# A two-layer kernel on one core: the skip term added by TensorE, more turns by DMA, and a new written order

## The chip, the cores and the metric

The kernel runs on one core of one Trainium2 chip. The metric is the device time of one execution in microseconds (us). Before the change three runs took 256.9 to 257.2, with a median of 257.14.

## The reference

Two kinds of layer alternate, twice each, on x of 2048 tokens by 512 channels (x starts as q). `LN` is a layer norm without weights.

```python
def A(q, k, v, shift_k, ssm_k, ssm_D):
    k_shift = sum(shift(k, t) * shift_k[:, t] for t in range(4))   # causal, 4 taps per channel
    kv = k_shift * v
    y = causal_conv(kv, ssm_k)          # per channel, length 2048, by FFT of 4096 points
    y = y + kv * ssm_D
    return q * y

def B(x, w1, b1, w2, b2):               # 512 -> 1376 -> 512
    return gelu(LN(x) @ w1 + b1) @ w2 + b2

for _ in range(2):
    x = x + A(LN(x), k, v, shift_k, ssm_k, ssm_D)
    x = x + B(LN(x), w1, b1, w2, b2)
```

k, v, the filter and D are the same in both A layers, so y is the same too: the kernel computes it once and keeps it.

## The kernel before

All of A's heavy work is in a first part of about 98 us; the rest is the four layers' norms and gates and two MLPs (`mm1` at L704, `mm2` at L738; four groups of four token tiles, two passes), which the change does not touch.

The first part computes the long convolution as a transform of 32 x 64 points by matmuls. Names of the steps, with c a group of 128 channels (0 to 3):

- `lk`, `lv`, `lK`, `lx` and others on S (SyncE's queue): loads. `lsT` brings the short filter's taps, `sF` (POOL) converts them, and `dg0` to `dg2` (L435, four operations each) make diagonal matrices `DG` from them.
- `kT0` to `kT3` (PE, L441) turn four blocks of k; `kT0e` to `kT3e` copy them out of PSUM.
- `kv{c}{o}` (PE, L524) apply the four taps by the diagonals for groups 0 to 2; `kvm` (DVE, L530) multiplies by v. Group 3 is done by POOL: `kg0` to `kg3` and `ka1` to `ka3` (L455, L457, L462), then `kgm` (L466).
- `s00` (statistics of the first four token tiles), `s01` (POOL, small) and `s02` (its normalisation, four operations): the first norm.
- `kd0`, `kd4` (L393): D is added to the filter's first tap, `Kd[:, :, 0]`, from `Dz`, for each half of the filter.
- `KS` (PE, L400, 16 blocks) and `K2` (PE, L413, 16 blocks) transform the filter; `sa`, `sb` (S) copy its halves to the other row order. Together the K stage.
- `U{c}S{q}` (PE, L325) is the first stage for kv, `U{c}T{h}` its turn: by PE and a copy (L357), or by a DMA transpose (L304), as the string `UT` says for each group (`P` or `X`).
- For each group and j from 0 to 3: `X` (PE, L558, second stage), `T` (DVE, L573, product with the filter), `V` (PE, L582, inverse second stage).
- `Z` (DMA transposes, L629) and `TC`, `TD` (PE, L617) turn the result, `Y` (PE, L649) is the last stage, and `g`, `h`, `p`, `b`, `LT0` gate, normalise and turn the first token tiles for the MLP.

A name with `e` is the emptying of that block's PSUM bank pair, by ACT (L237) or DVE (L239). PSUM has four such slots. What runs where, and in what order, is a list written out by hand, `ORDER`: `name.engine` and the slots taken (P for PE, D for VectorE, A for ScalarE, G for GpSimd, S for SyncE's queue). `_Plan.write` issues the steps in that order, so each engine and SyncE's queue work their own steps strictly in it. The costs and dependences in `plan.add` served to find the order; the semaphores follow from the memory that the issued instructions touch.

Of the kernel before, what the change touches and what calls it, by code (L numbers as in the profile page):

```python
# [28 lines left out]
sa0.S U2T0.P3 K27e.A K213.P2 K25e.A U2T1.P0 K213e.A sa1.S U1T0.P1 U2T0e.D B1.G sb1.S s11.G U2T1e.A sb3.S  # L29
U3S0.P22 sa3.S U1T0e.D U1T1.P3 U3S0e.A X20.P00 U1T1e.D U3S2.P1 X20e.A X10.P21 U3S2e.D X21.P32 X10e.A U3S3.P0  # L30
T20.D0 X21e.A U3S1.P1 U0T0.P2 lx.S U3S1e.A T10.D1 X13.P30 U3S3e.A V20.P10 U0T0e.D X13e.A U3T0.S X23.P01 T21.D2
U0T1.P2 V20e.A T13.D0 X00.P32 X23e.A V10.P11 U0T1e.D X00e.A V21.P0 V10e.A T23.D1 X01.P30 V13.P2 V21e.A T00.D2
X02.P11 X01e.A V23.P0 X02e.D V13e.A X03.P32 T01.D0 V23e.A V00.P1 X03e.A T02.D1 X11.P20 V01.P0 V00e.A T03.D2
X12.P31 X11e.A V02.P1 V01e.D X12e.A U3T1.S X30.P22 T11.D0 V02e.A V03.P0 X30e.A T12.D1 X22.P30 V11.P1 V03e.A
T30.D2 X31.P21 X22e.A Z01.S V12.P0 V11e.D X31e.A Z00.S T22.D0 X32.P32 V12e.A V30.P12 X32e.A T31.D1 Z10.S
X33.P20 V22.P0 X33e.A T32.D2 Z03.S V31.P3 V22e.A T33b.D0 V32.P2 Z13.S V31e.A T33a.D1 V33b.P0 V30e.D V32e.A
Z02.S V33a.P3 V33be.D V33ae.A TC0a.P1 TC0b.P2 Z12.S TC0ae.A TD0a.P3 TC1.P0 TC0be.D TD0ae.A Z11.S TD0b.P1
TC1e.D Y00.P2 TD0be.A TC3.P3 w3.S w1.S Y00e.A g00.D w2.S Y01.P1 TC3e.A w4.S TC2.P0 g01.D Y02.P2 h00.D Y01e.A
# [87 lines left out]
def kernel(ctx: ExitStack, tc: tile.TileContext, A_q, A_k, A_v, A_shift_k, A_ssm_k, A_ssm_D,  # L126
                 B_x, B_w1, B_b1, B_w2, B_b2, out):
    nc = tc.nc
    P = 128
# [166 lines left out]
    with tc.tile_pool(name="ps", bufs=1, space=bass.MemoryType.PSUM) as ps:  # L296
# [92 lines left out]
        for c in range(8):  # L389
            if c % (8 // NK) == 0:  # L390
                sl = slice(c * 16, c * 16 + P // NK)
                kd = plan.add(f"kd{c}", {"G": 300, "D": 130}, lK[c * NK // 8], lambda it, sl=sl: (
                    nc.vector if it["eng"] == "D" else nc.gpsimd).tensor_tensor(Kd[:, sl, 0], Kd[:, sl, 0], Dz[:, sl], ALU.add))  # L393
# [433 lines left out]
```

## Time and profile before

| | us |
|---|---|
| median of three runs | 257.14 |
| the profiled execution | 256.81 |
| its span, first to last instruction | 255.1 |
| TensorE busy | 236.8 |
| VectorE busy | 174.5 |
| ScalarE busy | 146.1 |
| GpSimd busy | 54.5 |
| first matmul of the MLP begins at | 97.9 |

In the rows that follow, `L393` is a line of the kernel, `out<-in` are tiles (nearly all of them lie in one big tile, `arena`), `x4` a count, and a bracket at the end tells how long the engine had been idle before and what ended that. A time alone is counted from the span's start. The granted clock is TensorE's, as a part of full speed.

### The profile page before, as it was taken

The page shows a single profiled execution, that of the slowest core. Times are in us where ns is not written, and L with a number is a line of the kernel's source. Part 1 is how long each engine was busy: PE and PEld are TensorE (multiplying, and loading weights), DVE is VectorE, ACT ScalarE, POOL GpSimd, SP SyncE. Part 2 cuts the span into 40 slices and gives each one's busy share as a digit, 9 for nine tenths or more (in the row PEclk, how much of TensorE's full clock was granted, in tenths as well). Part 3 has the DMA queues.
Part 4 walks back from the last instruction along what each step waited for, and adds up shares of the span by engine and source line. Part 5 has one row for each costly group of instructions (what it writes and reads, how often), then busy time and mean ns, then how long its engine had stood idle before and what let it go on. Part 6 is the DMA issues. An engine that isn't in the chain of part 4 may idle for free.

```text
span 255.1 us, 5088 instructions
## 1 busy us (share of the span) xinstructions
PE 236.8 (93%) x2084; PEld 146.3 (57%) x2084; DVE 174.5 (68%) x321; ACT 146.1 (57%) x210; POOL 54.5 (21%) x52
## 2 busy tenths in 40 slices
...
GB/s 132 382 334 167 222 442 180 76 320 321 312 135 103 148 237 288 3 0 82 5 82 0 78 6 20 62 0 82 4 1 165 0 11 157 0 14 71 1 20 63
DMA packets 53040, 30.15 MB, mean 118 GB/s; under 512 B 46642, under 2 KB 50456, under 8 KB 51736
## 3 DMA queue, kind: packets, MB, share of 16 engines
...
## 4 chain that ended last, share of the span: by engine, by line
PE 72%; DVE 12%; DMA 7%; issue 4%; ACT 2%; SPq 2%; ACTq 0%; DVEq 0%
PE po L738 30%; PE ph L704 29%; DMA arena<-in_A_v_dram 4%; DVE T L573 4%; DVE arena L239 3%; PE p L325 2%; PE p L357 2%; PE p L649 2%; DVE arena L393 2%; DMA arena<-in_A_ssm_D_dram 2%; PE p L400 2%; PE p L413 2%; PE p L524 1%; DVE ZT L239 1%; DMA arena<-ZT 1%
## 5 line engine op out<-in xcount | busy, mean ns | idle before, releaser
L706 ACT ACTIVATE arena<-ph,B 128x512 bf16<-128x512 f32 (+5 forms) x110 | 63.7, 604 | 81.1 <-PE ph L704 81.0
L704 PE MATMUL ph<-arena 128*128 128x512 bf16 (+4 forms) x440 | 78.5, 336 | 0.1
L738 PE MATMUL po<-arena 128*128 128x512 bf16 (+2 forms) x363 | 77.4, 373 | 0.0
L704 PEld LDWEIGHTS <-arena 128*128 128x128 bf16 (+1 forms) x440 | 40.4, 100 | 37.2 <-DMA arena<-in_B_w_dram 0.4
L738 PEld LDWEIGHTS <-arena 128*128 128x128 bf16 (+1 forms) x363 | 35.4, 98 | 40.5
L743 DVE TENSOR_TENSOR arena<-po,arena 128x512 bf16<-128x512 f32 (+1 forms) x33 | 21.5, 673 | 43.6 <-PE po L738 43.6
L237 ACT ACTIVATE arena<-p 128x1024 bf16<-128x1024 f32 (+5 forms) x38 | 37.8, 1071 | 10.1 <-PE p L441 3.9
L271 POOL TENSOR_TENSOR lrsm<-lrsm,mhalf 128x4 f32<-128x4 f32 (+2 forms) x10 | 8.9, 885 | 95.9 <-DVE lrsm L265 95.9
L237 ACT ACTIVATE ZT<-p 128x1024 bf16<-128x1024 f32 (+1 forms) x22 | 22.0, 1055 | 2.5 <-PE p L325 2.5
L259 DVE BATCH_NORM_STATS2 lstm<-arena 128x6 f32<-128x512 bf16 x32 | 19.9, 681 | 0.2
L573 DVE TENSOR_TENSOR T<-xb,arena 128x2048 bf16<-128x2048 bf16 (+1 forms) x17 | 18.7, 1159 | 0.0
L239 DVE CAST arena<-p 128x1024 bf16<-128x1024 f32 x15 | 17.7, 1223 | 1.4 <-PE p L400 0.9
L582 PE MATMUL p<-arena,T 128*128 128x128 bf16 x256 | 16.5, 219 | 1.0 <-DVE arena L239 0.4
L271 POOL TENSOR_TENSOR lrsg<-lrsg,mhalf 128x4 f32<-128x4 f32 x8 | 8.1, 1014 | 40.2 <-DVE lrsg L268 40.1
L237 ACT ACTIVATE xb<-p 128x1024 bf16<-128x1024 f32 x15 | 16.1, 1165 | 0.1
L582 PEld LDWEIGHTS <-T 128*128 128x128 bf16 x256 | 14.9, 98 | 1.6 <-issue 1.3
L455 POOL TENSOR_TENSOR T<-arena,SK 128x2048 bf16<-128x2048 bf16 (+3 forms) x4 | 14.9, 3740 | 3.8 <-ACT arena L237 3.7
L259 DVE BATCH_NORM_STATS2 lstg<-arena 128x6 f32<-128x512 bf16 x24 | 14.8, 679 | 0.0
L276 DVE TENSOR_SCALAR arena<-arena,lmvg,lrsg 128x512 bf16<-128x512 bf16 x28 | 9.7, 409 | 6.7 <-POOL lrsg L271 6.7
L239 DVE COPY arena<-p 128x2048 bf16<-128x2048 bf16 (+3 forms) x10 | 10.5, 1049 | 4.4 <-issue 3.0
L276 DVE TENSOR_SCALAR arena<-arena,lmvm,lrsm 128x512 bf16<-128x512 bf16 x32 | 11.2, 409 | 2.3 <-POOL lrsm L271 2.3
L524 PE MATMUL p<-DG,arena 128*128 128x128 bf16 x192 | 11.4, 219 | 1.2 <-ACT ZT L237 0.9
...
## 6 DMA issues: line engine op xcount, KB each, us to landing
...
arena<-tabM SPq DMA_DIRECT2D x1, 2048.0 KB, 12.1
arena<-in_A_q_dram SPq DMA_DIRECT2D x1, 2048.0 KB, 8.2
...
```

The costliest lines, as they stand in the source:

```text
L237: nc.scalar.activation(dst, src, AF.Copy)
L239: nc.vector.tensor_copy(dst, src)
L259: nc.vector.bn_stats(self.st[:, i, 0, :], x_t[:, GT * g + i, :] if src is None else src[:, i, :])
L271: nc.gpsimd.tensor_tensor(self.rs[:, a:b], self.rs[:, a:b], mhalf[:, a:b], ALU.pow)
L276: nc.vector.tensor_scalar(out=dst[:, i, :], in0=xs, scalar1=self.mv[:, i, 0:1], scalar2=self.rs[:, i:i + 1], op0=ALU.subtract, op1=ALU.mult)
L455: nc.gpsimd.tensor_tensor(m[:, t:NT, :], kn[:, 0:NT - t, c3], sk(t, NT - t), ALU.mult)
L573: eng.tensor_tensor(view(Tb[it["slot"]["T"]], [2, n, CW]), x2, kk, ALU.mult)
L582: nc.tensor.matmul(o[:, i, :], T[:, r, i, :], Mt[:, ka + i, 1 - r, :], start=r == 0, stop=r == 1)
L704: nc.tensor.matmul(o.rearrange("p (i t) -> p i t", t=P), W1t[:, ct, ft * P:ft * P + m], lt[:, a:b, ct, :], start=ct == 0, stop=ct == CT - 1)
L706: nc.scalar.activation(hT[0:m, ft, a * P:b * P], o, AF.Gelu_apprx_tanh, bias=B1[0:m, ft:ft + 1])
L738: nc.tensor.matmul(po[:, a:b], hT[0:m, ft, i * P:(i + 1) * P], W2t[0:m, ft, a:b], start=ft == 0, stop=ft == FT - 1)
L743: nc.vector.tensor_tensor(xs, po[:, a:b], xs, ALU.add)
```

## The change

1. `kd0` and `kd4` become two matmuls each on PE (identity by `Kd`'s column, identity by `Dz`, summed in PSUM) and an emptying back into `Kd`: `kd0e` on ACT, `kd4e` on DVE.
2. `UT` goes from `PPPX` to `PPXX`: group 2 of u is turned by two DMA transposes instead of 32 PE transposes and two copies.
3. The load of x, 2 MB, becomes four of 512 KB, `lr0` to `lr3`, later in SyncE's queue.
4. The weight loads' dependences in the plan name fewer products.
5. Some costs in the plan are changed (`kv` 1880, `s00` 6500 and `s02` 2900 on ACT).
6. The order is new throughout. Among other things `lsT` now stands behind the four loads of k, the blocks of k come as 1, 2, 0, 3 instead of 1, 3, 0, 2, `dg0` and `s02` change engine (ACT; DVE), and the groups of X, T and V come as 1, 0, 2, 3 instead of 2, 1, 0, 3. In the old list DVE's steps run, at the place that the prediction speaks of, `U2T0e U1T0e U1T1e U3S2e T20 T10 U0T0e T21 T13 U0T1e T23 T00 X02e T01 T02 T03 V01e T11 T12 T30 V11e T22 T31 T32 T33b T33a V30e V33be`, and SyncE's queue ends with `sa3 lx U3T0 U3T1 Z01 Z00 Z10 Z03 Z13 Z02 Z12 Z11 w3 w1 w2 w4`.

The old order is shown up to the filter's transform.

```diff
--- before.py
+++ after.py
@@ -16,28 +16,28 @@
 
 
 ORDER = """
-lSK.S lk1.S lsT.S lk3.S lk0.S lk2.S bSK.P0 lh1.S bSKe.A lh113.S lx0.S kT1.P1 lv0.S sF.G lv1.S dg0.D dg2.D
-kT1e.A lK00.S kT3.P2 dg1.D lK01.S kT0.P3 kT3e.A kT2.P0 kT0e.A kg0.G kT2e.D s00.A kv10.P1 kv21.P2 kvm10.D kg1.G
-U1S0.P30 kv11.P0 U1S0e.A kvm21.D U1S1.P1 kvm11.D kv00.P3 U1S1e.A s01.G lK10.S kv01.P2 kvm00.D ka1.G s02.A
-U0S0.P01 kvm01.D U1S3.P1 lK11.S kv20.P3 U1S3e.D U0S0e.A kd0.D U0S3.P2 kvm20.D KS11.P1 U0S3e.A KS21.P0 kg2.G
-lX.S KS11e.D KS10.P3 KS21e.A KS00.P2 KS10e.A U2S0.P02 KS00e.D KS30.P1 U2S0e.A U2S3.P3 KS30e.D U0S2.P2 U2S3e.A
-KS20.P0 lH.S lW.S U2S1.P1 U0S2e.A KS20e.D lM.S KS31.P3 ka2.G lx1.S U2S1e.A KS01.P2 kd4.D KS50.P0 KS31e.A
-KS01e.D KS70.P1 KS70e.A KS41.P3 KS50e.D KS61.P2 KS41e.A KS40.P1 KS61e.D KS60.P0 KS40e.A KS51.P3 kg3.G KS60e.D
-KS71.P2 KS51e.A U1S2.P1 KS71e.A U2S2.P0 U1S2e.D U0S1.P3 U2S2e.A K211.P2 U0S1e.D K29.P1 K211e.A K210.P0 K29e.D
-K28.P3 K210e.A K214.P2 ka3.G K28e.A K24.P1 K214e.D K21.P0 K24e.A K215.P3 sa2.S K21e.D sb2.S K212.P2 K215e.A
-K20.P1 K212e.D lb0.S K23.P0 K20e.A lb1.S K22.P3 K23e.D K26.P2 K22e.A kgm.G K25.P1 s10.D K26e.A K27.P0 sb0.S
...
+lSK.S lk1.S lk2.S lk0.S lk3.S lsT.S bSK.P0 lh1.S bSKe.A lx0.S lh113.S kT1.P1 lv0.S lv1.S kT2.P2 kT1e.A lK01.S
+kT0.P3 kT2e.A lK00.S kT3.P0 kT0e.D sF.G dg0.A dg2.D kT3e.D s00.A kg0.G dg1.D kv00.P1 kv10.P2 kvm00.D U0S0.P30
+kg1.G kvm10.D kv01.P0 U0S0e.A U1S0.P11 kvm01.D kv20.P2 U1S0e.A lK11.S U0S2.P3 s01.G kvm20.D kv11.P0 U0S2e.A
+U2S0.P12 lK10.S ka1.G kvm11.D U0S1.P2 U2S0e.A kv21.P3 s02.D U0S1e.A kd0.P0 U1S2.P1 kvm21.D kd0e.A U1S3.P2 lW.S
+U1S2e.A KS10.P0 U1S3e.D KS20.P3 kg2.G KS10e.A KS00.P1 KS20e.A KS30.P2 KS00e.D U2S3.P0 KS30e.A KS21.P3 U2S3e.D
+lX.S KS11.P1 lH.S KS21e.A KS31.P2 lM.S KS11e.D lx1.S KS01.P0 KS31e.A kd4.P3 kd4e.D KS01e.A ka2.G KS50.P1
+KS60.P3 KS50e.D KS51.P2 KS60e.A KS71.P0 KS51e.D KS41.P1 KS71e.A KS40.P3 KS41e.D KS61.P2 KS40e.A KS70.P0
+KS61e.D kg3.G U1S1.P1 KS70e.A U2S2.P3 U1S1e.A K20.P2 U2S2e.D K29.P0 K20e.A K22.P1 K29e.D K23.P3 K22e.A K21.P2
+K23e.D K27.P0 K21e.A K213.P1 K27e.A ka3.G K25.P3 K213e.D sb0.S K24.P2 sa0.S K25e.A K28.P0 K24e.D K26.P1 lb1.S
+K28e.A K212.P3 lb0.S K26e.D K211.P2 K212e.A K214.P0 s10.D K211e.A K210.P1 sb1.S sa1.S U1T0.P3 kgm.G K214e.A
+K215.P2 K210e.A U1T1.P0 K215e.A sa2.S U1T0e.D U2S1.P1 sb2.S U2S1e.A sb3.S U0S3.P2 U1T1e.D sa3.S X11.P30
+U0S3e.A B1.G U2T0.S X10.P11 s11.G X11e.D U3S0.P01 X10e.A X12.P22 U0T0.P3 T11.D0 X12e.A U3S0e.A U3S1.P1 U0T0e.D
+X13.P20 U3S1e.A U0T1.P0 T10.D1 X13e.A U3S2.P3 U3S3.P1 U0T1e.D U3S2e.A V10.P20 T12.D2 U3S3e.A X02.P01 V11.P3
+V10e.A T13.D1 X00.P12 U3T0.S X02e.A V12.P2 X00e.D V11e.A X01.P00 T02.D0 V13.P1 X01e.A T00.D2 V12e.A X03.P31
+X03e.A U2T1.S T01.D1 X20.P02 V00.P2 V13e.A X20e.D X21.P30 V00e.A Z10.S V02.P1 T03.D2 X21e.A V01.P0 T20.D0
+U3T1.S V02e.A X30.P21 V03.P3 T21.D1 X30e.A Z11.S X23.P12 V03e.A V01e.D V20.P22 X23e.A X31.P30 T30.D2 V21.P0
+Z01.S V20e.A T23.D0 X22.P11 X31e.A lr0.S V30.P21 Z00.S X22e.D V21e.A X32.P32 V30e.A T31.D1 V23.P0 X32e.A
+T22.D2 X33.P10 V31.P2 X33e.A T32.D0 V22.P3 V31e.A T33a.D1 V32.P1 V22e.A T33b.D2 V33a.P2 Z03.S V23e.D V32e.A
+V33b.P3 V33ae.D Z02.S V33be.A TC0b.P0 TC0a.P1 TD0a.P3 TC0be.D TC2.P2 TC0ae.A Z12.S TD0ae.A TD0b.P1 TC2e.A
+Y00.P0 Z13.S TD0be.D TC1.P3 Y00e.D g00.D w1.S Y01.P1 TC1e.A lr2.S TC3.P2 w4.S g01.D lr3.S Y20.P0 lr1.S h00.D
+w2.S Y01e.A Y10.P3 w3.S Y20e.A TC3e.D p00.G Y02.P1 Y10e.A b00.D Y30.P0 h01.D Y02e.A LT0.P2 Y12.P3 p01.G Y30e.A
+LT0e.D g02.D Y22.P1 Y12e.A Y32.P2 b01.D Y22e.A h02.D Y32e.D p02.G b02.D
 """
 NA, NB = 32, 64
 
@@ -238,7 +238,7 @@
         else:
             nc.vector.tensor_copy(dst, src)
 
-    UT = "PPPX"
+    UT = "PPXX"
     ZM = "XXPP"
     KSC, K2C = 440, 440
     EPS = 1e-5
@@ -389,8 +389,10 @@
         for c in range(8):
             if c % (8 // NK) == 0:
                 sl = slice(c * 16, c * 16 + P // NK)
-                kd = plan.add(f"kd{c}", {"G": 300, "D": 130}, lK[c * NK // 8], lambda it, sl=sl: (
-                    nc.vector if it["eng"] == "D" else nc.gpsimd).tensor_tensor(Kd[:, sl, 0], Kd[:, sl, 0], Dz[:, sl], ALU.add))
+                def mms(o, sl=sl):
+                    nc.tensor.matmul(o, IDt[:], Kd[:, sl, 0], start=True, stop=False)
+                    nc.tensor.matmul(o, IDt[:], Dz[:, sl], start=False, stop=True)
+                _, kd = mm_evac(f"kd{c}", 120, lK[c * NK // 8], mms, [P // NK], lambda sl=sl: Kd[:, sl, 0])
             for g in range(2):
                 def mms(o, c=c, g=g):
                     for m in range(8):
@@ -488,7 +490,7 @@
                 nc.scalar.activation(sm[:], sm[:], AF.Copy, scale=-1.0 / D)
                 for i in range(GT):
                     nc.scalar.activation(junk[:], x[:, i, :], AF.Square, bias=sm[:, i:i + 1], accum_out=sq[:, i:i + 1])
-            s0 = plan.add(f"s{n}0", {"D": 3190, "A": 4700}, [ld], stat)
+            s0 = plan.add(f"s{n}0", {"D": 3190, "A": 6500}, [ld], stat)
 
             def scale(it):
                 if s0["eng"] == "A":
@@ -506,7 +508,7 @@
                     return
                 for i in range(GT):
                     nc.scalar.activation(lna0[:, i, :], lna0[:, i, :], AF.Identity, bias=mr[:, i:i + 1], scale=S.rs[:, i:i + 1])
-            return s0, plan.add("s02", {"D": 1350, "A": 2200}, [s1], apply) if n == 0 else s1
+            return s0, plan.add("s02", {"D": 1350, "A": 2900}, [s1], apply) if n == 0 else s1
         _, s2 = first(0, lna0, lx0)
         s10, _ = first(1, x1, lx1)
         kvp, USp, ZU = [], [], []
@@ -522,7 +524,7 @@
                             tau = 8 * o2 + i - t
                             w = kT[:, cc, tau, 2:2 + P] if tau >= 0 else kT[:, cc, tau + NT, 1:1 + P]
                             nc.tensor.matmul(o[:, i, :], w, DG[:, cc, t, :], start=t == 0, stop=t == KS - 1)
-                pe = plan.add(f"kv{cc}{o2}", {"P": 1800}, kTe + [dg[cc]],
+                pe = plan.add(f"kv{cc}{o2}", {"P": 1880}, kTe + [dg[cc]],
                               lambda it, mms=mms: mms(view(pf[it["slot"]["ps"]], [8, P])), take=["ps"])
 
                 def mul(it, pe=pe, cs=cs, o2=o2):
@@ -539,7 +541,6 @@
               plan.add("lb1", {"S": 500}, [lM], lambda it: nc.sync.dma_start(
                   b1T[0:FL, FT - 1:FT], apf(B_b1, (FT - 1) * P, [[1, FL], [1, 1]])), dma=("copy", 2 ** 15))]
         plan.add("B1", {"G": 200}, lb, lambda it: nc.gpsimd.tensor_copy(B1[:], b1T[:]), rank=1)
-        lx = load("lx", x_t[:], q_d.rearrange(TOK, p=P), 2 ** 21, USp)
 
 
         Tcc, Xcc, Vcc, Vp = [], [], [], []
@@ -595,11 +596,13 @@
                     Vcc[cc].append(ev)
                     Vp.append(pe)
             zv.append(v0)
-        w1 = load("w1", W1t[:], B_w1.rearrange("(ct p) f -> p ct f", p=P), 1376 << 10, sum(Tcc, []))
-        wd = sum(Tcc, [])
-        w2 = load("w2", W2t[:, 0:FT - 1, :], B_w2[0:(FT - 1) * P, :].rearrange("(ft p) d -> p ft d", p=P), 1280 << 10, wd)
-        w3 = load("w3", W2t[0:FL, FT - 1, :], B_w2[(FT - 1) * P:F, :], 96 << 10, wd)
-        w4 = load("w4", W2t[FL:FL + 1, FT - 1, :], apf(B_b2, 0, [[D, 1], [1, D]]), 1024, wd)
+        lx = [load(f"lr{g}", x_t[:, GT * g:GT * g + GT, :], xd[:, GT * g:GT * g + GT, :], 2 ** 19, USp + Xcc[3][:2],
+                   rank=2 if g else 0) for g in range(4)]
+        w1 = load("w1", W1t[:], B_w1.rearrange("(ct p) f -> p ct f", p=P), 1376 << 10, sum((t[0:2] for t in Tcc), []))
+        wd, we = sum(Tcc, []), sum((t[1:3] for t in Tcc), [])
+        w2 = load("w2", W2t[:, 0:FT - 1, :], B_w2[0:(FT - 1) * P, :].rearrange("(ft p) d -> p ft d", p=P), 1280 << 10, we)
+        w3 = load("w3", W2t[0:FL, FT - 1, :], B_w2[(FT - 1) * P:F, :], 96 << 10, we)
+        w4 = load("w4", W2t[FL:FL + 1, FT - 1, :], apf(B_b2, 0, [[D, 1], [1, D]]), 1024, we)
 
 
         def zsrc(cc, off, dims):
@@ -673,7 +676,7 @@
                 ya = YA[0][:, a:b, :] if m == 2 else view(pf[y["slot"]["ps"]], [1, D])
                 nc.vector.tensor_tensor(ln, ln, ya, ALU.mult)
                 nc.vector.tensor_tensor(xs, xs, ln, ALU.add)
-            ga = plan.add(f"g0{a}", {"D": 1190 if m == 2 else 930}, [y, s2, lx], gate, free=yf)
+            ga = plan.add(f"g0{a}", {"D": 1190 if m == 2 else 930}, [y, s2, lx[0]], gate, free=yf)
             gs = stats(LM[0], 0, a, b, [ga], f"h0{a}")
             gp = plan.add(f"p0{a}", {"G": 700}, [gs], lambda it, a=a, b=b: LM[0].scale(a, b))
             gb = plan.add(f"b0{a}", {"D": 350 * m}, [gp], lambda it, a=a, b=b: LM[0].apply(lnx[0], 0, a, b))
```

More of the change, by code (lines that the diff above doesn't have):

```diff
@@ L29 @@
[L29 to L38, printed above, removed]
```

2 lines of the change are left out of this document (removed).

## The prediction

> **What bounds the kernel now.** I read the page's busy shares, then busy time by stage, then the chain that ended last, then the order of time on POOL and DVE. First the page and the stages (columns of a stage: length, then busy time and count of PE, weight loads, DVE, ACT, POOL, granted clock, DMA share, GB/s):
> ```profile
> span 255.1 us, 5088 instructions
> PE 236.8 (93%) x2084; PEld 146.3 (57%) x2084; DVE 174.5 (68%) x321; ACT 146.1 (57%) x210; POOL 54.5 (21%) x52
> ...
> 29.90:44.70 14.80, 12.32 (x286) 8.79 (x288) 12.94 (x11) 12.23 (x13) 14.49 (x6) 0.70 0.76 318
> 44.70:58.40 13.70, 13.46 (x200) 11.50 (x200) 12.35 (x17) 12.83 (x14) 3.46 (x3) 0.95 0.61 216
> 58.40:70.00 11.60, 11.51 (x186) 11.04 (x183) 11.56 (x11) 11.52 (x14) 0.00 (x0) 1.00 1.06 310
> 70.00:83.50 13.50, 12.54 (x215) 11.95 (x212) 13.50 (x13) 13.50 (x15) 0.00 (x0) 1.00 0.70 114
> 109.50:255.10 145.60, 142.65 (x672) 66.06 (x669) 89.38 (x213) 53.40 (x79) 13.09 (x13) 1.00 0.18 41
> ```
> PE's 93% is mostly the MLP half (142.65 of 145.60), which the change leaves alone. The first 98 us are another matter: from 58.4 to 83.5 DVE (25.06 of 25.10) and ACT are full, so DVE's list sets the length there; from 30 to 58 the two share the emptying of PSUM. The chain shows what delays that stage:
> ```profile
> 20.30 3.75 PE p L524 x64
> ...
> 26.43 3.45 DVE arena L393
> ...
> 29.93 0.66 PE p L400 x32
> ...
> 36.35 1.74 DVE arena L393
> ...
> 56.95 0.44 PE p L325 x4
> ```
> L393 is the addition of D (kd0, kd4), 128x64 elements. PE waits for it twice. Why so small an operation takes 3.5 us is seen in the order of time:
> ```profile
> 25.95 3.61 POOL L455 TENSOR_TENSOR T<-arena,SK 128x1792 bf16<-128x1792 bf16 x1
> 26.35 3.52 DVE L393 TENSOR_TENSOR arena<-arena,Dz 128x64 bf16<-128x64 bf16 x1
> 29.50 0.68 POOL L457 TENSOR_TENSOR T<-kh,SK 128x256 bf16<-128x256 bf16 x1
> 29.93 0.64 PE L400 MATMUL p<-Ft,arena 32*128 32x64 bf16 x32 [2.79 <-DVE arena L393]
> ...
> 34.40 3.37 POOL L455 TENSOR_TENSOR T<-arena,SK 128x1664 bf16<-128x1664 bf16 x1
> 36.35 1.73 DVE L393 TENSOR_TENSOR arena<-arena,Dz 128x64 bf16<-128x64 bf16 x1
> 38.13 0.78 PE L400 MATMUL p<-Ft,arena 32*128 32x64 bf16 x48 [1.58 <-DVE arena L393]
> ...
> 42.87 4.05 POOL L466 TENSOR_TENSOR arena<-arena,T 128x2048 bf16<-128x2048 bf16 x1
> ```
> Both end 0.3 us after the POOL instruction that was running when they came (29.87 against 29.56; 38.08 against 37.77), however long they had waited. So these DVE operations, which read SBUF and write SBUF, stood still until POOL's running instruction had ended. POOL runs such instructions nearly without a gap from 11.3 to 46.9, and the new order puts other DVE operations there. That decides this case.
>
> **The change, part by part.** Rows for the prices: groups with shapes kept apart; then order of time; then ACT's busy time over the K stage; then DMA issues (KB each, us to landing).
> ```profile
> L237 ACT ACTIVATE arena<-p 128x1024 bf16<-128x1024 f32 x28 | 27.4, 1065 | 4.6 <-PE p L400 3.3 <-PE p L413 0.8 <-PE p L649 0.4
> L276 DVE TENSOR_SCALAR arena<-arena,lmvg,lrsg 128x512 bf16<-128x512 bf16 x28 | 9.7, 409 | 6.7 <-POOL lrsg L271 6.7
> L706 ACT ACTIVATE arena<-ph,B 128x128 bf16<-128x128 f32 x20 | 5.6, 380 | 0.3 <-PE ph L704 0.2
> ```
> ```profile
> 1.63 0.42 SPq L301 DMA_DIRECT2D sT<-in_A_shift_k_dram  x1
> ...
> 3.71 2.44 SPq L301 DMA_DIRECT2D kh<-in_A_k_dram  x2
> 7.67 2.04 DVE L435 TENSOR_SCALAR DG<-IDt,sF 128x128 bf16<-128x128 bf16 x12 [7.67 <-POOL sF L382]
> 11.18 0.98 PEld L441 LDWEIGHTS <-arena 128*128 128x128 bf16 x12 [0.39 <-DMA arena<-in_A_k_dram]
> 11.31 7.95 POOL L455 TENSOR_TENSOR T<-arena,SK 128x2048 bf16<-128x2048 bf16 x2 [3.67 <-ACT arena L237]
> 12.44 0.96 DVE L239 COPY arena<-p 128x1536 bf16<-128x1536 bf16 x1 [2.72 <-issue]
> 12.66 3.75 PE L524 MATMUL p<-DG,arena 128*128 128x128 bf16 x64 [0.33 <-ACT arena L237]
> 21.80 4.07 POOL L462 TENSOR_TENSOR T<-T,T 128x2048 bf16<-128x2048 bf16 x1
> 21.87 2.93 ACT L508 ACTIVATE arena<-arena,am,lrsg 128x512 bf16<-128x512 bf16 x4 [0.71 <-POOL am L500]
> 55.56 1.23 DVE L239 COPY arena<-p 128x2048 bf16<-128x2048 bf16 x1 [0.32 <-issue]
> 63.60 9.95 SPq L304 DMA_TRANSPOSE arena<-ZT  x2
> ```
> ```profile
> 30.61:57.78 27.17, 24.43 (x25) 0.81 0.68 266
> ```
> ```profile
> arena<-in_A_q_dram SPq DMA_DIRECT2D x1, 2048.0 KB, 8.2
> ...
> kh<-in_A_k_dram SPq DMA_DIRECT2D x1, 84.0 KB, 7.8
> ...
> sT<-in_A_shift_k_dram SPq DMA_DIRECT2D x1, 4.0 KB, 4.6
> ```
> (1) *D by TensorE.* Each of two additions becomes two matmuls of 64 columns and one emptying of 64 columns. Between 0 (hidden) and 1.07 us (a whole 1024-column emptying); nearest is the 128x128 form, 0.38, so about 0.4 for the emptying and 0.4 for two matmuls. kd0 lies behind U1S2 and U1S3 on PE, so it costs nothing; for kd4 the next block on PE, KS50, waits: 0.8. Gone are the PE waits of 2.79 and 1.58.
>
> (2) *Start of kv.* In the new order kT3 is the last of the four turned blocks of k; the first products of a channel group read it (a negative tap reads the last tokens), while before the last was kT2, which they do not read. So kv00 waits for a copy as at 12.44 to end: 13.4 against 12.66, +0.75.
>
> (3) *PE up to the first KS block.* Six kv blocks at 1.88 (3.75 for two) and seven U blocks at 0.44 from 13.4 give 27.8; with kd0 and hand-overs 28.2, against 29.93. That is 1.7 less, with seven U blocks behind it instead of four.
>
> (4) *K stage.* Before, ACT worked off 25 emptyings in 27.17, the waits for L393 among them: 1.09 each. The new order gives ACT 23 and a short one between kd0e and K215e: from 27.1 on 25.4, so 52.5. The last K2 block on PE must be done one emptying and a hand-over (1.4) before that, and behind it stands DVE's first copy of turned u: 51.0 instead of 55.56. The two copies of U2, one on DVE and one on ACT, that lay there are gone. Parts 1 to 4 together: -4.6.
>
> (5) *U2 turned by DMA.* DVE's list from its first copy of turned u: four copies, 17 products and six full emptyings of X and V; before five copies, the same products and five emptyings. One copy (1.23) has gone for one emptying (1.2), so the stage keeps its 29 us. SP takes two more transposes. Two took 9.95 on SP (4 to 6 us each) beside the x load, which is now away. From 53 on, four of these and a Z turn need 20 us, to about 75; X32 wants the last at about 75. I take 0; up to +2 if it is late, and the cover is only DVE's backlog.
>
> (6) *x in four loads, weights after fewer products.* Nothing: in SP's queue w1 stands one turn earlier than before and behind lr0 only; w2 comes three quarter loads later but is read first at 109. Without that cover, three quarters of the x load (8.2), some 6 us, would be exposed. B1 and LT0 as before.
>
> (7) *The diagonals, and s02, under POOL.* Before, sT landed at 6.2 (1.63 + 4.6), and all 12 diagonal operations ran from 7.67 to 9.7 while POOL had nothing. Now lsT is issued behind all four k loads. The nearest row is kh, the load that stood behind them: issued at 3.71, landed 7.8 later, 11.5. sF on POOL follows then, and right behind it in POOL's queue kg0 (4.07), whose k has landed by 11.2. dg2 on DVE stands behind kT0's copy (ends about 11.8), so kg0 is running when dg2 comes. Behind dg2 on DVE wait kT3e, dg1 and kvm00, and for kT3e wait all kv blocks.
> Price: 0 if a tensor-scalar does not care for POOL. The nearest row in kind and place is L393 (DVE, SBUF to SBUF, in the same stretch), which did; copies and products that read PSUM (12.44, beside POOL's 11.31 to 19.26) did not, but these diagonals read and write SBUF. So I take the wait, and since the diagonals follow one another every 0.17 us (2.04 for 12), sooner than one ends, I let all four pass in one gap. kg0 11.6 to 15.7; dg2 to 16.5; kT3e to 17.4; POOL's next (3.88) 16.5 to 20.4; dg1, come at 17.4, 20.4 to 21.2; kv10 at 21.2 instead of 15.3: +5.9. s02, four tensor-scalars now on DVE, comes at about 31.3, where POOL's 1792 instruction ends at 31.4: nothing here, else up to 4 us, since kvm21 is behind it and KS20 needs the bank that kvm21 frees.
>
> The Trainium skill, "SBUF — State Buffer", section "Who interferes with whom", says that a DVE instruction with two SBUF inputs waits for a reading GpSimd one (as L393 did), and that `tensor_scalar` in a two-port mode is blocked too. By that rule the sum holds +5.9; by L393's row read strictly, as a matter of two inputs, it would be without it, 252.2. No run here shows a tensor-scalar beside POOL.
>
> **Sum.** 255.1 - 4.6 + 5.9 = 256.4, and 1.7 outside the span (the profiled execution took 256.81) gives 258.1. The median of the runs, 257.14, is 0.3 above the profiled one: 258.4.
>
> **The rivals.**
> *A. Diagonals and s02 do not wait.* Then only parts 1 to 6 stay: 255.1 - 4.6 + 1.7 = 252.2, up to 254 with late turns, and 250.5 if the K stage, with three U blocks in it instead of eight, loses less to the granted clock of 0.70 seen from 29.9 to 44.7. For it: before shows no tensor-scalar waiting. Against it: L393. This is the one on the other side; it decides if dg1 has ended by 15.3.
> *B. They wait, but dg2 comes first.* If sT lands late enough that DVE is already free, dg2 starts 0.03 after sF (7.44 + 0.20, then 7.67), ahead of kg0. kg0 then runs 12.3 to 16.4, dg1 17.1; kv10 1.8 late, and s02 perhaps 1.4: 255.4.
> *C. One operation per gap.* POOL's next instruction was under way 0.06 us before its predecessor's end (29.50 against 29.56), so it may take its turn between two of DVE's. dg2's four pass at 15.7, 19.6, 20.1 and 20.3, kT3e ends at 21.4, dg1 among the small POOL operations of s01 at best at 22.8, else after ka1 at 26.9: +7.5 to +11.8. s02 waits for the running one and three more (3.61 + 0.68 + 4.06 = 8.35), less some 2 us of slack: +6 to +10. 252.2 + 16 = 268, between 262 and 273. For it: L457 lost nothing visible to L393. Against it: the overlap of the diagonals.
> In the same section the skill says that whichever starts first gets the pair for its whole instruction and the other fully blocks. Applied to each instruction by itself that is C; no run here shows it.
>
> **Chances.** Forecast 0.34, A 0.22, B 0.14, C 0.30. The range 251.5 to 270 leaves out about 0.08 of A at the bottom and 0.10 of C at the top; the forecast's own range is 256 to 260. A change under 0.2% (0.5 us) can hardly be told from none here. Faster: A, B and a small part of the forecast, 0.38; within 0.2%: 0.04; slower: 0.58.
>
> **What would show it.** Right: diagonal rows of DVE that begin near 11.8 and last until a POOL instruction ends; the first L524 block at 17 instead of 12.66; L393 gone, and no PE wait of 2.8 before the first L400; DVE's first copy of turned u near 57. Wrong by A: twelve short diagonals by 14 and that copy near 51. Wrong by C: single diagonals 4 us apart, and s02's four operations spread over 8 us. Wrong in part 5: PE waiting for a DMA from ZT before X blocks of groups 2 and 3. Wrong in part 6: weight loads of L704 waiting for B_w by more than the 0.4 of before.

## The result, and the profile after

The changed kernel takes 267.12 us (median of 4 runs, 266.99 to 269.0) against 257.02 for the kernel before: a ratio of 1.041 with a 95% interval of 1.036 to 1.046. It is slower by 10 us. (Runs over 1.5% above the fastest of their kernel are in the medians below, but not in the ratios.) The single time forecast was 258.4; the time that came is that of rival C (268).

The first view is the page of the kernel after, its span and its busy shares.
```profile
span 265.5 us, 5049 instructions
PE 235.9 (89%) x2056; PEld 146.3 (55%) x2056; DVE 185.0 (70%) x320; ACT 143.8 (54%) x209; POOL 54.5 (21%) x52
```
PE's work is down by 0.9 us, ACT's by 2.3 and POOL's is unchanged. DVE is the odd one: one instruction fewer than before and 10.5 us more of busy time. That is, in the main, time in which DVE stood still inside an instruction. The order of time on DVE after shows which (start, length, engine, line, operation, count; the second and third rows are the first one and the first two of the fourth row's group, and 38.20 is the last one of the group at 33.07):
```profile
9.85 0.96 DVE L239 COPY arena<-p 128x1536 bf16<-128x1536 bf16 x1 [9.85 <-PE p L443]
10.76 4.14 DVE L437 TENSOR_SCALAR DG<-IDt,sF 128x128 bf16<-128x128 bf16 x1
10.76 7.95 DVE L437 TENSOR_SCALAR DG<-IDt,sF 128x128 bf16<-128x128 bf16 x2
10.76 8.49 DVE L437 TENSOR_SCALAR DG<-IDt,sF 128x128 bf16<-128x128 bf16 x4
19.18 0.94 DVE L239 COPY arena<-p 128x1536 bf16<-128x1536 bf16 x1
20.04 0.73 DVE L437 TENSOR_SCALAR DG<-IDt,sF 128x128 bf16<-128x128 bf16 x4
...
33.07 9.33 DVE L276 TENSOR_SCALAR arena<-arena,lmvg,lrsg 128x512 bf16<-128x512 bf16 x4
38.20 4.20 DVE L276 TENSOR_SCALAR arena<-arena,lmvg,lrsg 128x512 bf16<-128x512 bf16 x1
42.32 1.21 DVE L532 TENSOR_TENSOR arena<-p,arena 128x1024 bf16<-128x1024 f32 x1
```
And POOL's over the same stretch (the second row is the first one of the third row's group):
```profile
10.53 0.20 POOL L382 CAST sF<-sT 128x16 f32<-128x16 bf16 x1 [3.61 <-DMA sT<-in_A_shift_k_dram]
10.76 4.09 POOL L457 TENSOR_TENSOR T<-arena,SK 128x2048 bf16<-128x2048 bf16 x1
10.76 7.89 POOL L457 TENSOR_TENSOR T<-arena,SK 128x2048 bf16<-128x2048 bf16 x2
18.61 0.43 POOL L459 TENSOR_TENSOR T<-kh,SK 128x128 bf16<-128x128 bf16 x1
...
19.61 1.04 POOL L271 TENSOR_TENSOR lrsg<-lrsg,mhalf 128x4 f32<-128x4 f32 x1
...
29.69 4.07 POOL L464 TENSOR_TENSOR T<-T,T 128x2048 bf16<-128x2048 bf16 x1
33.83 3.37 POOL L457 TENSOR_TENSOR T<-arena,SK 128x1664 bf16<-128x1664 bf16 x1
37.16 0.96 POOL L459 TENSOR_TENSOR T<-kh,SK 128x384 bf16<-128x384 bf16 x1
38.20 4.04 POOL L464 TENSOR_TENSOR T<-T,T 128x2048 bf16<-128x2048 bf16 x1
```
Lay the two lists side by side. The first diagonal of dg2 ends at 14.90, with POOL's first product (14.85); the second at 18.71, with the second product (18.65). The four of s02 begin while POOL's 29.69 runs, and then POOL has its 3.37, its 0.96 and its 4.04 before the last of the four ends at 42.40. Each of these instructions of POOL, the one of 0.96 included, lets one tensor-scalar of DVE pass. The four of dg1 come at 20.04, beside POOL's 128x4 operations, and take 0.73 together.

What that does to PE, and where the K stage then ends (order of time of the kernel after, PE and then DVE's first copy of turned u):
```profile
20.27 4.96 PE L526 MATMUL p<-DG,arena 128*128 128x128 bf16 x63 [8.84 <-DVE arena L239]
...
35.50 0.40 PE L402 MATMUL p<-Ft,arena 32*128 32x64 bf16 x16
43.58 1.74 PE L402 MATMUL p<-Ft,arena 32*128 32x64 bf16 x48 [7.68 <-DVE arena L532]
...
65.83 2.35 DVE L239 COPY arena<-p 128x2048 bf16<-128x2048 bf16 x2
```
PE begins the kv blocks in earnest at 20.27 instead of 12.66, makes up 2.0 of these 7.6 us until the first KS block (35.50 instead of 29.93), and then stands 7.68 us for kvm21, which stood behind s02 on DVE. The rest of the K stage takes 22.65 us (65.83 - 35.50 - 7.68) where before it took 25.63 (55.56 - 29.93): 2.98 less. The sum is 7.6 - 2.0 + 7.7 - 3.0 = 10.3, and DVE's first copy of turned u is 10.3 us late. From that copy to the end of the span it is 199.7 us, before 199.5: the stretch behind it takes as long as it did.

A smaller loss goes with the first wait. The 63 matmuls of the row at 20.27 take 4.96 us; in runs 2 to 5 below, which lack that wait, the same 63 take 3.68. The granted clock was 0.50 from 20.27 to 22.50 and 0.91 from there to 25.10, and 1.00 in runs 2 to 5. What lowered it isn't tested here.

This gives the landmarks by which all runs below are read, each from the order of time of that kernel's profiled run (us):

| kernel | kv blocks begin | first KS block | PE waits for s02 | first copy of turned u | from there to the end |
|---|---|---|---|---|---|
| before | 12.66 | 29.93 | - | 55.56 | 199.5 |
| after | 20.27 | 35.50 | 7.68 | 65.83 | 199.7 |
| s02 on ACT | 21.27 | 37.92 | - | 61.42 | 199.7 |
| diagonals early | 15.52 | 29.48 | 7.85 | 59.98 | 199.6 |
| both | 15.49 | 30.55 | - | 53.66 | 199.6 |
| both, taps on ACT's queue | 12.15 | 27.81 | - | 51.70 | 199.6 |
| POOL's products left out | 13.75 | 27.71 | - | 51.50 | 199.7 |
| D by TensorE alone | 12.93 | 27.72 | - | 51.99 | 200.1 |

### The profile page after: what moved, and what is told of

Read it like the earlier page. It is cut to its first block, busy times and chain, and to the rows that moved or that the text cites. A ratio compares the mean times of both kernels' runs of the same rounds, so it can differ in the third digit from the quotient of the medians.

```text
span 265.5 us, 5049 instructions
## 1 busy us (share of the span) xinstructions
PE 235.9 (89%) x2056; PEld 146.3 (55%) x2056; DVE 185.0 (70%) x320; ACT 143.8 (54%) x209; POOL 54.5 (21%) x52
## 4 chain that ended last, share of the span: by engine, by line
PE 71%; DVE 13%; issue 3%; ACT 3%; DMA 2%; SPq 0%; DVEq 0%
PE po L741 29%; PE ph L707 28%; DVE arena L239 5%; PE p L526 5%; PE p L325 3%; DMA arena<-ZT 2%; DVE arena L276 2%; DVE T L574 2%; PE p L415 1%; PE p L357 1%; PE p L402 1%; ACT arena L237 1%; PE p L583 1%; PE p L620 1%; ACT ZT L237 1%
## 5 line engine op out<-in xcount | busy, mean ns | idle before, releaser
L237 ACT ACTIVATE ZT<-p 128x1024 bf16<-128x1024 f32 (+1 forms) x24 | 24.3, 1060 | 11.1 <-PE p L325 11.0
L276 DVE TENSOR_SCALAR arena<-arena,lmvg,lrsg 128x512 bf16<-128x512 bf16 x32 | 19.0, 655 | 6.7 <-POOL lrsg L271 6.7
L526 PE MATMUL p<-DG,arena 128*128 128x128 bf16 x192 | 13.0, 231 | 9.1 <-DVE arena L239 8.8
L526 PEld LDWEIGHTS <-arena 128*128 128x128 bf16 x192 | 12.4, 105 | 9.4 <-POOL lmvg L498 9.3
L239 DVE COPY arena<-p 128x2048 bf16<-128x2048 bf16 (+3 forms) x10 | 9.5, 956 | 11.4 <-PE p L443 9.8
L239 DVE CAST arena<-p 128x1024 bf16<-128x1024 f32 (+2 forms) x15 | 16.4, 1130 | 1.5 <-PE p L402 0.7
L402 PE MATMUL p<-Ft,arena 32*128 32x64 bf16 x256 | 7.5, 233 | 8.9 <-DVE arena L532 7.7
L259 DVE BATCH_NORM_STATS2 lstg<-arena 128x6 f32<-128x512 bf16 x24 | 14.8, 678 | 0.0
```

The source lines that it names most:

```text
L237: nc.scalar.activation(dst, src, AF.Copy)
L239: nc.vector.tensor_copy(dst, src)
L259: nc.vector.bn_stats(self.st[:, i, 0, :], x_t[:, GT * g + i, :] if src is None else src[:, i, :])
L276: nc.vector.tensor_scalar(out=dst[:, i, :], in0=xs, scalar1=self.mv[:, i, 0:1], scalar2=self.rs[:, i:i + 1], op0=ALU.subtract, op1=ALU.mult)
L526: nc.tensor.matmul(o[:, i, :], w, DG[:, cc, t, :], start=t == 0, stop=t == KS - 1)
```

## The experiments

**1. Is it s02?** The theory: s02's four operations, one for each POOL instruction, cost what lies in PE's wait of 7.68. Moved to ACT they cost nothing there.
```diff
- ... kv20.P2 U1S0e.A lK11.S U0S2.P3 s01.G kvm20.D ... kv21.P3 s02.D U0S1e.A ...
+ ... kv20.P2 U1S0e.A lK11.S U0S2.P3 s01.G s02.A kvm20.D ... kv21.P3 U0S1e.A ...
```


> The changed kernel with s02 alone put back on ACT. Theory W (each DVE operation from SBUF to SBUF waits for one POOL instruction): the 7.7 us for which PE waits before KS20 go, ACT gets 2.9 us of work, mostly in its gaps: about 260 (258 to 262). Rival O (the new order itself is what costs, through its K stage at half clock, late turns and the order of groups; the waits are absorbed): within 1 us of 267.

Measured: 262.94 (ratio 1.022, 1.019 to 1.025). DVE's diagonals and PE in this run, in order of time:
```profile
11.78 8.48 DVE L437 TENSOR_SCALAR DG<-IDt,sF 128x128 bf16<-128x128 bf16 x4
...
21.27 6.27 PE L526 MATMUL p<-DG,arena 128*128 128x128 bf16 x63 [8.54 <-DVE arena L239]
...
37.92 1.15 PE L402 MATMUL p<-Ft,arena 32*128 32x64 bf16 x48
```
The wait of 7.68 has gone: 48 matmuls of the first KS blocks run together where the kernel after had 16 and then the wait. The gain is 4.2 and not 7, so the time lies above the expected 258 to 262. In this run the taps were converted 1.0 later (11.54 against 10.53), dg2 came 1.0 later (11.78 against 10.76), and the 63 matmuls of kv took 6.27 instead of 4.96; so the first KS block came 2.4 later. (The clock row of this profile reads 1.00 there, so why they are slow stays open.) The K stage took 23.5 instead of 22.65. 7.68 - 2.42 - 0.85 = 4.41, which is how much sooner the first copy of turned u is.

**2. Is it the place of the diagonals?** The load of the taps goes back to second place in SP's queue, and dg2 and dg1 stand ahead of the copies of kT0 and kT3 on DVE, so that they run before POOL's first product. s02 stays on DVE.
```diff
- lSK.S lk1.S lk2.S lk0.S lk3.S lsT.S bSK.P0 ... kT1.P1 lv0.S ...
+ lSK.S lk1.S lsT.S lk2.S lk0.S lk3.S bSK.P0 ... kT1.P1 sF.G dg2.D dg1.D lv0.S ...
- kT0.P3 kT2e.A lK00.S kT3.P0 kT0e.D sF.G dg0.A dg2.D kT3e.D s00.A kg0.G dg1.D kv00.P1 ...
+ kT0.P3 kT2e.A lK00.S kT3.P0 kT0e.D dg0.A kT3e.D s00.A kg0.G kv00.P1 ...
```


> The changed kernel with lsT back behind the first load of k and dg2, dg1 ahead of DVE's first copy, so that they run before kg0; s02 stays on DVE. W: the kv blocks begin 8 us earlier (about 12.3 instead of 20.3), s02 still spreads over four POOL instructions: about 259 (257 to 262). O: within 1 us of 267.

Measured: 260.9 (ratio 1.013, 1.009 to 1.017). In order of time:
```profile
7.12 1.39 DVE L437 TENSOR_SCALAR DG<-IDt,sF 128x128 bf16<-128x128 bf16 x8 [7.12 <-POOL sF L382]
...
27.05 9.49 DVE L276 TENSOR_SCALAR arena<-arena,lmvg,lrsg 128x512 bf16<-128x512 bf16 x4
...
37.73 1.74 PE L402 MATMUL p<-Ft,arena 32*128 32x64 bf16 x48 [7.85 <-DVE arena L532]
```
Eight diagonals take 1.39 us, 0.17 each, where four took 8.49. s02 meets POOL as before and PE waits for it again, 7.85.

**3. Both.** Edits 1 and 2 together; if the two waits are all that the change lost, this is rival A's kernel.

> Both of the two edits, everything else of the change kept. W: 252.2 (250.5 to 254), the prediction's rival A, and both gains add up. O: above 257, no better than before the change.

Measured: 255.21 (ratio 0.992, 0.989 to 0.995), faster than the kernel before, which rival O ruled out, but 3 us over what was expected and outside that range. The table says where: from the first KS block (30.55) to the first copy of turned u (53.66) it is 23.1 us, for 22.8 in the prediction's working, but kv begins at 15.49 instead of 13.4. The last block of k was late; the weight loads of the turning of k, of after and of this run, in order of time:
```profile
10.15 0.67 PEld L443 LDWEIGHTS <-arena 128*128 128x128 bf16 x12 [0.51 <-DMA arena<-in_A_k_dram]
```
```profile
9.69 1.20 PEld L443 LDWEIGHTS <-arena 128*128 128x128 bf16 x12 [2.62 <-DMA arena<-in_A_k_dram]
...
13.07 1.03 PEld L443 LDWEIGHTS <-arena 128*128 128x128 bf16 x12 [0.35 <-DMA arena<-in_A_k_dram]
```
The last of the four is read at 13.07 instead of 10.15, and the gap of 2.62 lies where the taps are in the queue, between the first and the second block of k. So the small load of the taps ahead of three loads of k may be a price of its own, which run 4 tests. Its size varies: with the taps in that place the last block is read at 13.20 in run 2 and at 11.95 in run 7, and with the taps behind all of k at 9.86 to 11.16 (the kernel after, runs 1, 5 and 6).

**4. The taps out of that queue.** "Both", with the taps' load issued on ACT's queue at the start.
```diff
+     nc.scalar.dma_start(sT[:], A_shift_k.rearrange("(ct p) k -> p ct k", p=P))
...
-         lS = [load("lsT", sT[:], A_shift_k.rearrange("(ct p) k -> p ct k", p=P), 2 ** 17),
+         lS = [plan.add("lsT", {"S": 400}, [], lambda it: None),
```


> The kernel with both waits undone, and the load of the taps issued on ACT's DMA queue at the start instead of second on SyncE's. In the trace of both, the four loads of k stood 2 to 3 us later than in the changed kernel (last turn of k at 13.1 instead of 10.2), with the 512 pieces of 8 bytes of the taps between them. If that is what keeps both at 255.2 instead of the predicted 252.2, kv begins 2 us earlier: about 253.2 (252.3 to 254). If the loads are late for another reason: no change, within 0.6 of 255.2.

Measured: 253.0 (ratio 0.987, 0.981 to 0.993). The same kernel was run again beside run 10:

> The same kernel as both_taps_actq, once more beside actq_k2_last on the same chip: 253.0 (252.6 to 253.4), as a base for it.

Measured: 252.81 (ratio 0.981, 0.978 to 0.985). In order of time, from the first of the two runs, the diagonals on DVE, POOL's first product, the last block of k and the kv blocks on PE:
```profile
8.88 1.39 DVE L438 TENSOR_SCALAR DG<-IDt,sF 128x128 bf16<-128x128 bf16 x8 [8.88 <-POOL sF L383]
10.19 1.82 DVE L240 COPY arena<-p 128x1536 bf16<-128x1536 bf16 x2
...
10.15 7.94 POOL L458 TENSOR_TENSOR T<-arena,SK 128x2048 bf16<-128x2048 bf16 x2 [1.30 <-DMA arena<-in_A_k_dram]
...
10.03 0.84 PE L444 MATMUL p<-IDt,arena 128*128 128x128 bf16 x12 [0.18 <-DMA arena<-in_A_k_dram]
...
12.15 3.68 PE L527 MATMUL p<-DG,arena 128*128 128x128 bf16 x63 [0.72 <-DVE arena L240]
```
k is in time again, and the diagonals end at 10.27, when POOL's first product has just begun. The two copies from PSUM behind them take 0.9 us each beside that product, as one does in run 5 with POOL idle (0.94 at 12.66). This kernel keeps the change except for the places of s02, of two groups of diagonals and of one load, and it is faster than the kernel before and the kernel after.

**5. The other side: POOL away.** In place of moving DVE's work, POOL's long instructions are taken out of the changed kernel.
```diff
+             if t == 0:
+                 nc.gpsimd.memset(ksum, 0.0)
+             return
...
-                 kg.append(plan.add(f"ka{t}", {"G": 4100}, kg[-1:], lambda it: nc.gpsimd.tensor_tensor(ksum, ksum, kpart, ALU.add)))
+                 kg.append(plan.add(f"ka{t}", {"G": 4100}, kg[-1:], lambda it: None))
```


> The changed kernel, its order untouched, with POOL's tap products kg0 to kg3 and sums ka1 to ka3 left out (the sum is set to zero, so channel group 3 of kv is not computed). W: with nothing running on POOL, the diagonals take 0.7 us for four and s02 1.4 us where they stand, kv begins near 12.5, and the time falls by 13 to 15: about 253 (251.5 to 255). O: the order's own cost stays, above 262.

Measured: 253.01 (ratio 0.984, 0.981 to 0.987). DVE and POOL, in order of time:
```profile
10.76 1.98 DVE L437 TENSOR_SCALAR DG<-IDt,sF 128x128 bf16<-128x128 bf16 x4 [0.32 <-POOL sF L382]
13.53 0.73 DVE L437 TENSOR_SCALAR DG<-IDt,sF 128x128 bf16<-128x128 bf16 x4
25.28 1.37 DVE L276 TENSOR_SCALAR arena<-arena,lmvg,lrsg 128x512 bf16<-128x512 bf16 x4
```
```profile
10.67 1.81 POOL L458 MEMSET T<- 128x2048 bf16 x1
...
20.89 4.06 POOL L471 TENSOR_TENSOR arena<-arena,T 128x2048 bf16<-128x2048 bf16 x1
```
DVE's instructions stand where the new order put them; POOL's are missing, but for one product that ends at 24.95, before s02 comes. dg2 takes 1.98 instead of 8.49, s02 1.37 instead of 9.33. Even the one memset holds dg2: 1.98 where dg1 took 0.73. 267.1 - 253.0 = 14.1 us is what POOL's missing instructions cost the changed kernel, and run 4 reaches the same 253.0 with all of them in place. The table divides the loss: against this run, kv begins 6.5 later in the kernel after, the stretch to the first KS block is 1.3 longer (the 63 slower matmuls), PE waits 7.7 for s02, and the rest of the K stage is 1.1 shorter; that is 14.3 at the first copy of turned u. So the two waits, with the slower matmuls behind the first, are the loss.

**6. One wait for each instruction?** If each DVE instruction pays one POOL instruction, fewer instructions pay less, even if each does more work. From run 1 (s02 on ACT), a group's four diagonals become one tensor-tensor of 512 elements.
```diff
+                 if it["eng"] == "D":
+                     nc.vector.tensor_tensor(DG[:, ct, :, :], apf(IDt, 0, [[P, P], [0, KS], [1, P]]),
+                                             apf(sF, ct * KS, [[CT * KS, P], [1, KS], [0, P]]), ALU.mult)
+                     return
```


> s02_on_act with the four diagonals of a group made by one DVE instruction (a product with two SBUF inputs, 512 elements) instead of four. If each instruction waits for one POOL instruction: dg2 waits once (4.1) instead of twice (8.0), the copy of kT3 ends some 3 us earlier, then dg1 waits once; kv10 comes about 2.5 earlier: about 260.4 (259 to 261.5) beside 262.9. If the wait belongs to the stretch and not to the instruction: no change, within 0.7 of 262.9.

Measured: 254.85 (four runs: 253.2, 253.3, 256.4 and 257.7; ratio 0.989, 0.982 to 0.996). The profile is of the run of 257.7. In order of time:
```profile
10.78 4.35 DVE L433 TENSOR_TENSOR DG<-IDt,sF 128x512 bf16<-128x512 bf16 x1
...
15.92 3.49 DVE L433 TENSOR_TENSOR DG<-IDt,sF 128x512 bf16<-128x512 bf16 x1
```
Each of the two waits once: dg2 takes 4.35 instead of 8.48. kv begins at 16.14 instead of 21.27, 5.1 earlier, where 2.5 was expected, and that is the whole difference between the profiled runs of this kernel and of run 1 (257.71 and 262.82; the first copy of turned u is 5.1 earlier, 56.28 for 61.42). The direction is what "one wait for each instruction" says, and the size was put too low; the operation changed as well as the count, so the run doesn't separate the two. The runs of 253 have no trace, and what they gained beyond 5.1 stays open. POOL waits too: its first two products take 8.37 together (7.89 in run 1) and the 128x128 behind them 0.90 (0.42 there).

**7. U2 turned by TensorE again.** From "both", to price part 5: the two turns go back to PE, with their emptyings on DVE and ACT, set among the blocks of the X stage.
```diff
- UT = "PPXX"
+ UT = "PPPX"
...
- ... U2T0.S ... U2T1.S ...
+ ... U0T1e.D U2T0.P0 U2T0e.D ... V10e.A U2T1.P1 U2T1e.A ...
```


> The kernel with both waits undone, and group 2 of u turned by PE again (32 transposes, a copy of 1.22 on DVE and one of 1.9 on ACT) in place of two DMA transposes. The prediction's part 5 (DVE's list sets the X stage; the turns by DMA are in time): one more copy on DVE, 255.2 + 1.2 = 256.4 (255.7 to 257.5). Rival (the late turns, 6.3 us from issue to landing and on the chain at 83 to 89 of the changed kernel, cost more than the copy): 255.2 or less, down to 254.

Measured: 261.0 (ratio 1.015, 1.012 to 1.019); 5.8 more than "both", all of it behind the first copy of turned u (53.29; 205.6 us from there, against 199.6). Both expectations put it too low. The size is not the copy alone; in order of time:
```profile
62.99 1.23 DVE L239 COPY arena<-p 128x2048 bf16<-128x2048 bf16 x1 [1.25 <-PE p L357]
...
68.76 0.70 PE L559 MATMUL p<-arena,Wt 128*128 128x128 bf16 x8 [1.97 <-ACT arena L237]
69.56 1.23 DVE L239 CAST xb<-p 128x1024 bf16<-128x1024 f32 x1 [3.07 <-PE p L559]
```
DVE, full in that stage otherwise, idles 1.25 and 3.07 us at the places where the turns were put. So 4.3 of the 5.8 are waits of this place, and the pure price of turning U2 by PE stays open. Without them the time would be about 256.7 by estimate (261.0 - 4.3), still above 255.2, so nothing here speaks for the rival, by which the late DMA turns cost more than the copies.

**8. D by TensorE alone.** The kernel before, with its own order, and only the additions of D replaced.
```diff
- ... U1S3e.D U0S0e.A kd0.D U0S3.P2 kvm20.D ... KS01.P2 kd4.D KS50.P0 ...
+ ... U1S3e.D U0S0e.A kd0.P0 U0S3.P2 kd0e.A kvm20.D ... KS01.P2 kd4.P1 kd4e.D KS50.P0 ...
```


> The kernel before with only D's addition moved to TensorE (kd0e on ACT, kd4e on DVE), in the old order. By the prediction's part 1: PE's waits of 2.79 and 1.58 go and 0.8 comes: 257.0 - 3.6 = 253.4 (252.5 to 255). Rival: the waits are taken up by the emptying that follows, which is full anyway, and the gain is only DVE's time, (3.5 + 1.7 - 0.4) over two engines, less: 255 to 257.

Measured: 253.99 (ratio 0.988, 0.985 to 0.991). The first KS block starts at 27.72 instead of 29.93 and the first copy of turned u is 3.57 earlier; the stretch behind it is 0.6 longer (200.1 for 199.5). The time lies below the rival's 255 to 257. So this part is worth 3.1 us by itself, and the new order without its two waits (252.8 to 253.0) adds about 1 us to that.

**9. Part 2: kT3 last.** The kernel before with the third and the last turned block of k exchanged.
```diff
- lSK.S lk1.S lsT.S lk3.S lk0.S lk2.S ... kT3.P2 dg1.D lK01.S kT0.P3 kT3e.A kT2.P0 kT0e.A kg0.G kT2e.D ...
+ lSK.S lk1.S lsT.S lk2.S lk0.S lk3.S ... kT2.P2 dg1.D lK01.S kT0.P3 kT2e.A kT3.P0 kT0e.A kg0.G kT3e.D ...
```


> The kernel before with the names of token blocks 2 and 3 of k exchanged in its order, so that kT3 is loaded and turned last, as in the new order; nothing else. By part 2 of the prediction the first kv block then waits for the last copy of a turned block: 13.4 instead of 12.66, and the time is 0.75 higher: 257.9 (257.6 to 258.2) where before takes 257.1. Rival: the first blocks of kv have slack, since PE waits for DVE and ACT behind them: 257.1, no difference.

Measured: 258.07 against 257.56 of the kernel before measured beside it (ratio 1.0025, 1.0002 to 1.0047): 0.6 us, with 0.05 to 1.2 as bounds. In order of time:
```profile
13.59 0.29 PE L524 MATMUL p<-DG,arena 128*128 128x128 bf16 x1
13.78 0.96 DVE L239 COPY arena<-p 128x1536 bf16<-128x1536 bf16 x1 [5.15 <-ACT arena L237]
14.88 5.31 PE L524 MATMUL p<-DG,arena 128*128 128x128 bf16 x56 [1.00 <-DVE arena L239]
```
One matmul of kv starts, and the rest wait for the last copy, as the prediction said. The size isn't a test of its 0.75, though. kv starts in earnest 2.2 later (14.88 for 12.66; the last block of k, too, is read later, at 12.21 for 11.18), and its first 63 matmuls take 5.70 (64 took 3.75). But PE's first wait for L393 falls from 2.79 to 1.06, and the first copy of turned u is only 0.77 later (56.33 for 55.56). So the rival's slack is there as well, and the 0.6 is what is left after it.

**10. The same the other way round.** Run 4 with kT2 last.
```diff
- lSK.S lk1.S lsT.S lk2.S lk0.S lk3.S ... kT2.P2 kT1e.A lK01.S kT0.P3 kT2e.A lK00.S kT3.P0 kT0e.D dg0.A kT3e.D ...
+ lSK.S lk1.S lsT.S lk3.S lk0.S lk2.S ... kT3.P2 kT1e.A lK01.S kT0.P3 kT3e.A lK00.S kT2.P0 kT0e.D dg0.A kT2e.D ...
```


> both_taps_actq with the token blocks of k loaded and turned in the order 1, 3, 0, 2, as before the change, so that the last turned block is one that the first products of kv do not read. By part 2 of the prediction kv starts 0.75 us earlier against the last copy of a turned block: 252.3 (251.7 to 252.9) where both_taps_actq took 253.0. Rival: kv waits for the diagonals or the last load anyway, or the stage behind it is held by the emptying of PSUM, and nothing is gained: 253.0.

Measured: 257.9, with 12 runs from 252.6 to 262.0; too wide a spread to price 0.75 us, so it decides nothing on part 2. Its profiled run (256.8) shows one thing that can happen in this kernel. In order of time:
```profile
9.92 0.20 POOL L383 CAST sF<-sT 128x16 f32<-128x16 bf16 x1
...
11.23 8.00 POOL L458 TENSOR_TENSOR T<-arena,SK 128x2048 bf16<-128x2048 bf16 x2 [1.11 <-ACT arena L238]
```
```profile
10.15 5.30 DVE L438 TENSOR_SCALAR DG<-IDt,sF 128x128 bf16<-128x128 bf16 x8 [10.15 <-POOL sF L383]
...
11.29 4.16 DVE L438 TENSOR_SCALAR DG<-IDt,sF 128x128 bf16<-128x128 bf16 x1
```
The taps were converted 1.3 us later than in run 4 (9.92 against 8.65 there). Seven diagonals passed; the eighth began 0.06 us after POOL's product and took 4.16 instead of the 0.25 of its sisters. 1.3 us of lateness became 4 (kv begins at 16.37 instead of 12.15). Why the taps came late there, and what set the times of the other eleven runs, isn't settled.

## Why the prediction was right or wrong

**The mechanism was right, and the step that failed is in part 7.** The prediction took the wait of the tensor-scalars under POOL, against L393's row read strictly, and that is what decided the sign. It then wrote "I let all four pass in one gap". The runs show one for each of POOL's tap instructions: dg2 8.49, kT3e's end at 20.1 instead of 17.4. The reason given, that diagonals followed one another every 0.17 us, was a fact about diagonals with POOL idle; POOL's next instruction is ready at its predecessor's end and takes its turn too, which 29.50 against 29.56 in the prediction's own rival C had shown.

In the forecast's terms the first copy of turned u was to come at 56.9 (51.0 + 5.9); it came at 65.83. Of these 8.9 us only 1.4 arose before the first KS block (35.50 for 28.2 + 5.9 = 34.1). There two errors offset each other, which is luck: kT3e ended 2.7 later than forecast, but dg1, which was to wait until 20.4, met only POOL's 128x4 operations and ended at 20.77, before the forecast's 21.2. In this stretch the 63 slower matmuls alone took 1.3 more than in run 5 (4.96 for 3.68), a term that the prediction doesn't have. The rest is s02. So the direction was right, the forecast's own range of 256 to 260 was missed by 7, and the stated range held because it made room for rival C.

**The same step made s02 free.** "s02: nothing here" rested on its arrival at a gap at 31.3. It arrived at 33.07, under an instruction that ended at 33.76, and stood for the three that followed: 9.33 where run 5 took 1.37, so 7.96 of waiting, of which PE saw 7.68, where the prediction had nothing, and 4 at most. Rival C had it at 8.35 less 2 us of slack; the slack was 0.3. Runs 1 and 2 take the two waits away one at a time, 3 and 4 take both, and 5 takes POOL away instead.

**Rival C's arithmetic** gave 268, and its mechanism is the one that the rows show (kT3e at 21.4 there, 20.1 measured, and dg1 "among the small POOL operations of s01", measured at 20.04). The sum is near partly by luck: 252.2 + 16, where run 5 and the kernel after make it 253.0 + 14.1. The rule of the Trainium skill ("SBUF — State Buffer", section "Who interferes with whom") that whichever starts first keeps the pair of SBUF ports, shared by VectorE and GpSimd, for its whole instruction, applied to each instruction by itself, agrees with the rows of after (14.90 against 14.85), and with run 10's eighth diagonal, 0.06 us too late.

**Part 1** was right in place and roughly in size: kd's two matmuls took 0.27 and 0.21, its emptying 0.46 in the kernel after, where 0.4 and 0.4 were taken:
```profile
34.39 0.27 PE L393 MATMUL p<-arena,IDt 128*128 128x64 bf16 x1
34.48 0.21 PE L394 MATMUL p<-Dz,IDt 128*128 128x64 bf16 x1
...
34.73 0.46 ACT L237 ACTIVATE arena<-p 128x64 bf16<-128x64 f32 x1 [0.43 <-PE p L394]
```
Net, 3.57 was expected from the terms (2.79 + 1.58 - 0.8), and the first copy of turned u came 3.57 sooner in run 8; the time fell by 3.1.

**Part 2** named the right wait (run 9), but its 0.75 isn't shown: in run 4 and its repetition, with kT3 last, kv began at 12.15 and 12.71, about as early as before (12.66), and run 9's 0.6 is the remainder of a larger delay. **Part 3**, 14.8 us from the first kv block to the first KS block, took 15.2 in the kernel after, and from 14.0 (runs 2 and 5) to 16.7 (run 1). **Part 4**, 22.8 from there to the first copy of turned u, took 22.65 in the kernel after and up to 23.9 (run 4). Parts 1 to 4 together were -4.6; run 4 and its repetition are 4.2 and 4.8 below the kernel before measured beside them. In run 4 part of that agreement is luck: kv begins 1.25 earlier than the 13.4 of part 2, and parts 3 and 4 take 2.0 longer than forecast.

**Part 5** (nothing) and **part 6** (nothing) hold: 199.5 us from the first copy of turned u to the end before, 199.6 or 199.7 in the six kernels of the table that have these parts. In the chain of the kernel after a turn does end late:
```profile
83.17 6.28 DMA arena<-ZT
...
89.50 0.62 PE p L559 x8
```
PE begins at 89.50 when the turn has landed, so the sign that the prediction named against part 5 does show; but PE's wait there is 0.3 us, and the stretch is no longer than before. The weight loads of L704, which waited 0.4 for B_w before, don't wait for it in the kernel after. The price of the alternative is bounded by run 7, not measured.

**Rival A** named the time of a kernel without the waits, 252.2: run 4 measured 253.0, and 252.8 when repeated. **Rival B** did not occur: kg0 followed sF in POOL's queue at once, and dg2, though it began at the same 10.76, was the one that waited.
